# A two-branch gated attention kernel: the row maxima split on VectorE alone, one tile of memory results, other planned times and another order table

## The chip, the cores and the metric

The kernel runs on one NeuronCore of a Trainium2 chip, as one launch. The metric is the device time of an execution in microseconds. The time before is the median of three runs.

## What is computed

Two branches, A and B, with weights of their own, work on the same input x of 2048 tokens by 640 columns (all in fp32). A gate per token mixes their results. Each branch is an attention of 32 heads with 20 columns a head. The tokens are cut into four segments of 512. Inside a segment a head does causal softmax attention; from the segments before, it reads a compressed memory. The core of one branch, cut:

```python
for s in range(4):                       # segments of 512 tokens
    logits = qs @ ks.T * 20 ** -0.5 + mask        # causal
    a_dot = softmax(logits) @ vs
    a_mem = (phi(qs) @ M) / (phi(qs) @ z + 1e-6)
    outs.append(g * a_mem + (1 - g) * a_dot)      # g: one number per head
    M = M + phi(ks).T @ vs
    z = z + sum(phi(ks))
return concat(outs) @ wo
...
gate = sigmoid((x * gate_w).sum(-1))
return gate * A(x) + (1 - gate) * B(x)
```

Here phi(t) is t + 1 for positive t and exp(t) otherwise.

## The kernel before

**Windows and quads.** A window t (0 to 7) is one segment of one branch: segment t // 2, branch t % 2. Its 32 heads are worked on in eight quads of four heads; quads are numbered i = 8 t + u, 64 in all. The names that follow are those of the profile's tiles.

**Products in two parts.** The products by wq, wk, wv and wo need more precision than one pass of TensorE (PE) in its fast fp32 form gives. Each operand is split into a high part (a rounded copy) and a low part (the difference), and three products are summed. Inputs of 64 rows are used, so that the two halves of PE's array work on different matmuls at a time. These matmuls are line 773.

**Scores twice.** For each quad the scores are made in two layouts. S units (`s_unit`, matmuls at line 1209) make them with queries on partitions; VectorE (DVE) adds the causal mask and takes the maximum of each row (line 1196, into the tile `mx`). T units (`t_unit`, matmuls at line 1299) make them with keys on partitions; the maximum goes in as two more rows of the operands, so that ScalarE (ACT) only has to take the exponential (line 1291), after which GpSimd (POOL) clears the block on the diagonal (line 1292). The weighted sum of the values is `pv_unit` (line 1319, 32 matmul records a quad).

**From the maxima to the T units.** When the ten groups of maxima of a quad are there, `m_unit` makes a tile `mt` of 16 + 16 columns: a rounded copy (ACT, line 1220) and the difference (POOL, line 1221). `mrow_unit` transposes it on PE (line 1234), ACT copies it out (line 1251), and two DMAs on the queue of SyncE (SP, line 1246) put it into the last rows of the query operand `qst`. Only then may the quad's T units run.

**From a quad to the output.** The sums of a quad go to DRAM (`dots`). When the eight quads of a window are there, they come back in a layout by head columns: `reciprocals` makes the weights of the rows (line 1379 on DVE, then two reciprocals at line 1384), and `mix` multiplies each of the five pieces by them, on DVE (line 1429) or on POOL (line 1430), whichever the planner thinks free first. For windows 2 to 7 the result of the memory has been written by `mem_unit` into a tile `O` (PE line 883, then three DVE instructions at lines 897, 899 and 900). `o_transpose` turns it (PE line 925) and DVE adds it to the weighed piece (line 1496). The sum is split into two parts (ACT line 1420, then DVE line 1422 or POOL line 1423) and goes into the product by wo. Window 7 does this last part in another way: its quads are turned and weighed one by one (`fin_unit`). A tile `O` is given back when its five transposes are done; there are two of them. `update_unit` adds a window's keys and values to the memory, after that window's memory results have been read.

**Row tiles.** Most tiles of 128 x 512 come from one pool of NBIG = 29 rows (`big`). A T unit may start when there is room for its exponentials: in ten tiles of their own, or in this pool beyond a reserve.

**The order.** The order of all instructions is fixed while the program is made. The kernel's Python code holds a planner: a clock, a queue by priority for each of ACT (A), DVE (D), POOL (G) and SP (S), and a planned duration for each instruction. A line such as `put("D", 0.9, emit, then, prio=2)` says: on DVE, planned for 0.9 us, when done call `then`. `anyof` puts a piece of work on the engine whose queue is the shorter. PE's order comes out of the same clock: a unit is placed when the planner thinks its inputs there. On the chip each engine runs its instructions in the planned order and waits on semaphores wherever reality is later.

**The table.** `RULES` has an entry for a quad i where anything changes: the order of the quad's five S and five T units, then seven numbers that `rules` reads as span (the stretch over which they are spread), calm (the load of DVE up to which late units may start), lag, room (the reserve for exponentials), hold (how much earlier the quad starts), wait and wait2. The numbers hold until the next entry that changes them.

Of the kernel before, what the change touches and what calls it, by code (L numbers as in the profile page):

```python
# [12 lines left out]
F32 = mybir.dt.float32  # L13
# [3 lines left out]
ALU = mybir.AluOpType  # L17

P = 128
D = 640  # L20
S = 2048
# [3 lines left out]
L = 512  # L25
KT = D // P
NB = L // P
# [10 lines left out]
def r32(ap):  # L38
    return ap.bitcast(F32)
# [3 lines left out]
def tile_gated_mix_infini_attn(  # L43
# [17 lines left out]
    nc = tc.nc  # L61
# [7 lines left out]
    sb = ctx.enter_context(tc.tile_pool(name="sb", bufs=2))  # L69
# [18 lines left out]


    RULES = {  # L90
# [60 lines left out]
    }  # L151
    rule = {}
    DONE = {"A": 0.27, "D": 0.26, "G": 0.22, "S": 0.0}
# [46 lines left out]
    def put(e, dur, emit, then=None, prio=5):  # L200
        heapq.heappush(ready[e], (prio, next(seq), dur, emit, then))
        load[e] += dur
        start_next(e)
# [184 lines left out]
    gcol = [const.tile([P, 1], F32, name=f"gcol{b}") for b in range(2)]  # L388


    NBIG, NWST, NWH, SPARE = 29, 3, 4, 2
    VN = D // 2
    bank = Store([ps.tile([P, L], F32, name=f"bank{i}") for i in range(8)])

# [308 lines left out]
    def by_head(t, o):  # L703
        return o.rearrange("p n (h e) -> p n h e", e=DH) if t == 7 else o.rearrange("p n (c h e) -> p n h c e", c=KT, h=H)

    O_store = Store([sb.tile([P, NB, D], F32, tag=f"O{i}", name=f"O{i}", bufs=1) for i in range(2)])
    OTs = {}
    pqTs = {}
    arrived = set()
# [505 lines left out]
    def m_unit(i):  # L1215

        mt = sb.tile([P, 2, 2, 2 * NB], F32R, tag="mt32", name=f"mt{i}", bufs=3)
        m = mx[i].rearrange("p f a n -> p f (a n)")
        mts[i] = mt
        put("A", 0.11, lambda: nc.scalar.copy(mt[:, :, 0, :], m), lambda: put(  # L1220
            "G", 0.18, lambda: nc.gpsimd.tensor_tensor(
                out=mt[:, :, 1, :], in0=m, in1=r32(mt[:, :, 0, :]), op=ALU.subtract),
            lambda: m_ready(i), prio=0), prio=1)

    def m_ready(i):
        m_done.add(i)
        later(0, 0.2, lambda: True, lambda: mrow_unit(i))
# [148 lines left out]

    def reciprocals(t, d, g):
        def gates():
            put("D", 0.9, lambda: nc.vector.scalar_tensor_tensor(
                out=r32(d), in0=r32(d), scalar=gcol[t % 2], in1=r32(g), op0=ALU.mult, op1=ALU.mult), lambda: half(0), prio=2)  # L1380

        def half(c):
            cols = slice(L // 2 * c, L // 2 * (c + 1))
            put("D", 1.78, lambda: nc.vector.reciprocal(r32(d[:, cols]), r32(d[:, cols])),
                (lambda: half(1)) if c == 0 else done, prio=2)
            if c == 0:
                big.give(g)

        def done():
            inverse[t] = d  # L1390
            for fn in waiting.pop(t, []):
                fn()

        landed = then_all(2, gates)
        b = t % 2
        dma(0.8, lambda: nc.sync.dma_start(
            out=r32(d), in_=lanes_of(t)[:, DH:DH + 1, :].to_broadcast([H, 4, L])), landed, prio=-1, lat=1.2)
        dma(0.8, lambda: nc.sync.dma_start(
            out=r32(g), in_=rowg[t // 2][NB * b:NB * b + NB, :].rearrange("n p -> (n p)")[None, :].to_broadcast([P, L])), landed, prio=-1, lat=1.2)
# [4 lines left out]
    def mix(t, k, y):  # L1404
        def weighed():
            weighed_of[t] = weighed_of.get(t, 0) + 1
            if weighed_of[t] == KT:
                big.give(inverse.pop(t))
            if t < 2:
                parts()  # L1410
            else:
                mixed[t, k] = y
                later(1, 0.44, lambda: all(
                    (t, n, h) in mem_done for n in range(NB) for h in range(2)), lambda: o_transpose(t, k, parts))

        def parts():
            big.want((F32R, F32R), two_parts, prio=2)

        def two_parts(hi, lo):
            put("A", 0.515, lambda: nc.scalar.copy(hi, r32(y)), lambda: anyof(  # L1420
                2, lambda: (big.give(y), OTs.__setitem__((t, k), (hi, lo))),
                D=(0.85, lambda: nc.vector.tensor_tensor(out=lo, in0=r32(y), in1=r32(hi), op=ALU.subtract)),  # L1422
                G=(1.25, lambda: nc.gpsimd.tensor_tensor(out=lo, in0=r32(y), in1=r32(hi), op=ALU.subtract))), prio=2)

        def weigh():
            r = inverse[t]
            anyof(
                2, weighed,
                D=(0.9, lambda: nc.vector.tensor_tensor(out=r32(y), in0=r32(y), in1=r32(r), op=ALU.mult)),  # L1429
                G=(1.4, lambda: nc.gpsimd.tensor_tensor(out=r32(y), in0=r32(y), in1=r32(r), op=ALU.mult)))  # L1430

        def landed():
            if t in inverse:
                weigh()
            else:
                waiting.setdefault(t, []).append(weigh)

        dma(0.82, lambda: nc.sync.dma_start(out=r32(y), in_=lanes_of(t)[:, 4 * k:4 * k + 4, :]), landed, prio=0, lat=1.2)
# [353 lines left out]
```

## Time and profile before

| | |
|---|---|
| median of three runs | 1015.88 us (1014.32 to 1016.97) |
| the profiled execution's own time | 1016.54 us |
| its span, first to last instruction | 1014.8 us |
| PE, matmuls | 1002.1 us busy, 11260 matmuls |
| DVE | 769.3 us busy, 2604 instructions |
| ACT | 659.5 us busy, 1341 instructions |
| POOL | 612.3 us busy, 1040 instructions |
| mean granted clock of PE | 0.995 |
| DMA | 241.99 MB, 238 GB/s |

How to read the lines of it: times are in us unless marked ns. A group of instructions has the line of the kernel, the engine, the operation, the tiles it writes and reads (numbers left out), the shape and the count; then the busy time and the mean of one in ns; then the idle time of the engine just before them, with what ended most of it. The view of one line gives the least, the median and the largest duration in ns, and the first and the last start. In the timeline, a row has its start, its length, engine and line; the square bracket is the idle time before it and what ended it. PEld are weight loads, which run beside matmuls. Two matmuls run at a time, one in each half of the array, so PE counts as busy when only one of the halves is.

### The profile page before, as it was taken

What the parts mean: (1) busy time and instruction counts of PE and PEld (TensorE: products, weight loads), DVE (VectorE), ACT (ScalarE), POOL (GpSimd) and SP (SyncE); (2) the same over time, 40 slices, a digit from 0 to 9 for tenths busy, and PEclk for the clock granted to TensorE, in tenths of its full rate; (3) what the DMA queues carried; (4) which work ended last, traced back from release to release, by engine and by line L of the source; (5) the groups of instructions that cost most, each with busy time, mean ns of one, the idle gap of its engine ahead of it and who ended that gap; (6) DMA issues with size and microseconds to landing.
All of it is one profiled execution on the core that took longest, in us unless ns stands there. A gap on an engine that the chain in (4) does not pass through costs nothing.

```text
span 1014.8 us, 30827 instructions
## 1 busy us (share of the span) xinstructions
PE 1002.1 (99%) x11260; PEld 855.5 (84%) x11260; DVE 769.3 (76%) x2604; ACT 659.5 (65%) x1341; POOL 612.3 (60%) x1040
## 2 busy tenths in 40 slices
PE   9999999999999999999999999999999999999998
PEld 7998888888888888878888878897889888878876
DVE  4688777976787778877578976888567897689764
ACT  5376776776566767757766666675676666675672
POOL 4465657676476655775646656486675656567571
PEclk9999999999999999999999999998999999999999
DMA  7999989898896988866768687795876979688531
GB/s 248 308 306 270 298 255 305 274 283 259 262 286 185 286 237 245 268 183 219 237 177 300 188 267 234 206 301 175 252 230 182 313 213 281 206 228 267 151 93 62
DMA packets 148886, 241.99 MB, mean 238 GB/s; under 512 B 13216, under 2 KB 46144, under 8 KB 148416
## 3 DMA queue, kind: packets, MB, share of 16 engines
q1 hardware_dynamic: 148736, 240.03, 77.2%
q8 instruction: 89, 1.46, 0.6%
q14 instruction: 61, 0.50, 0.2%
HBM read 150.83 MB, written 94.65 MB: 242 GB/s over the span
## 4 chain that ended last, share of the span: by engine, by line
PE 84%; DMA 6%; DVE 5%; ACT 1%; POOL 1%; issue 1%; SPq 1%; ACTq 0%; DVEq 0%; POOLq 0%
PE bank L773 50%; PE bank L1319 13%; PE bank L1299 7%; PE bank L1209 7%; PE bank L883 3%; PE bank L965 3%; PE bank L925 2%; DMA row<-dots 1%; DMA dots<-row 1%; DMA kd<-row 1%; DVE bank L1196 1%; PE bank L1234 1%; DVE row L1429 1%; DVE row L1422 1%; DMA row<-in_xT_dram 1%
## 5 line engine op out<-in xcount | busy, mean ns | idle before, releaser
L1196 DVE CUSTOM_DVE_ANT_0 bank<-bank,tri 128x256 f32<-128x256 f32 (+3 forms) x1024 | 474.7, 520 | 150.2 <-PE bank L1209 96.8
L773 PE MATMUL bank<-row,wh 64*128 64x512 f32 x2308 | 498.6, 403 | 0.6 <-DVE mw L897 0.6
L1291 ACT ACTIVATE p<-bank 128x512 f32<-128x512 f32 x588 | 324.0, 601 | 140.0 <-PE bank L1299 108.4
L1292 POOL TENSOR_SCALAR_AFFINE_SELECT p<-p 128x256 f32<-128x256 f32 (+1 forms) x588 | 219.2, 380 | 228.6 <-ACT p L1291 219.2
L773 PEld LDWEIGHTS bank<-row,wh 64*128 64x128 f32 x2308 | 319.8, 186 | 11.8 <-issue 1.1
L773 PE MATMUL bank<-row,wl 64*128 64x512 f32 x1154 | 293.3, 402 | 0.0
L543 POOL TENSOR_TENSOR wl<-wst,wh 128x640 fp32r<-128x640 f32 x115 | 181.3, 1581 | 58.1 <-ACT wh L541 51.7
L1209 PE MATMUL bank<-kst,qst 60*128 60x384 f32 (+3 forms) x1024 | 184.0, 317 | 1.8 <-DVE row L1349 0.8
L773 PEld LDWEIGHTS bank<-row,wl 64*128 64x128 f32 x1154 | 173.6, 186 | 5.0 <-issue 0.6
L1299 PE MATMUL bank<-qst,kst 62*128 62x128 f32 (+3 forms) x1024 | 176.4, 317 | 1.0 <-ACT vst L1015 0.5
L773 PE MATMUL bank<-wvh,row 64*128 64x320 f32 x1280 | 176.7, 312 | 0.0
L1319 PE MATMUL bank<-p,vst 128*32 128x384 f32 (+3 forms) x1936 | 148.9, 431 | 0.0
L773 PEld LDWEIGHTS bank<-wvh,row 64*128 64x128 f32 x1280 | 147.4, 185 | 1.0 <-issue 0.2
L1196 DVE DVE_READ_ACCUMULATOR2_ANT mx<- 128x1 f32 x1024 | 144.6, 141 | 0.0
L1209 PEld LDWEIGHTS bank<-kst,qst 60*128 60x128 f32 x1024 | 137.5, 186 | 8.2 <-DVE row L1349 1.2
L1299 PEld LDWEIGHTS bank<-qst,kst 62*128 62x128 f32 x1024 | 130.5, 186 | 7.3 <-DVE mx L1196 1.0
L1319 PEld LDWEIGHTS bank<-p,vst 128*32 128x32 f32 x1936 | 59.3, 110 | 87.4 <-issue 62.7
L541 ACT CAST wh<-wst 128x640 fp32r<-128x640 f32 x119 | 86.4, 741 | 20.2 <-PE bank L773 14.4
L773 PE MATMUL bank<-wvl,row 64*128 64x320 f32 x640 | 99.3, 310 | 0.0
L1349 ACT COPY row<-bank 128x512 f32<-128x512 f32 x61 | 36.0, 590 | 79.4 <-PE bank L1319 71.1
L773 PEld LDWEIGHTS bank<-wvl,row 64*128 64x128 f32 x640 | 80.0, 185 | 0.6 <-issue 0.4
L518 POOL TENSOR_TENSOR wvl<-wst,wvh 128x640 fp32r<-128x640 f32 (+1 forms) x48 | 64.0, 1338 | 17.3 <-ACT wvh L515 17.3
(117 smaller groups left out, 1213.5 us busy)
## 6 DMA issues: line engine op xcount, KB each, us to landing
qst<-qd SPq DMA_DIRECT2D x128, 240.0 KB
kst<-kd SPq DMA_DIRECT2D x128, 240.0 KB
qd<-row SPq DMA_DIRECT2D x40, 512.0 KB
kd<-row SPq DMA_DIRECT2D x40, 512.0 KB
dots<-row SPq DMA_DIRECT2D x56, 256.0 KB
wst<-wmix SPq DMA_DIRECT2D x35, 320.0 KB
row<-dots SPq DMA_DIRECT2D x42, 256.0 KB
qd<-row SPq DMA_DIRECT2D x40, 256.0 KB
```

The source lines that it names most:

```text
L518: put("G", 0.77 * n, lambda: nc.gpsimd.tensor_tensor(out=wl[:, a:b, :], in0=w3, in1=r32(wh[:, a:b, :]), op=ALU.subtract), end, prio=4)
L541: put("A", 0.625, lambda: nc.scalar.copy(wh, w3), lambda: put(lo_eng, lo_cost, lambda: lo.tensor_tensor(out=wl, in0=w3, in1=r32(wh), op=AL ...
L543: lambda: lo.tensor_tensor(out=wl, in0=w3, in1=r32(wh), op=ALU.subtract), end, prio=3), prio=6)
L773: return nc.tensor.matmul(bank_of, lhsT=w[ROWS[half]], rhs=x_[ROWS[half]], start=start, stop=stop)
L883: return nc.tensor.matmul(pm[:, a - h0:c - h0, :].rearrange("p h e -> p (h e)"), lhsT=r32(pqTs[t, m][ROWS[half], P * n:P * (n + 1)]), rhs= ...
L1196: put("D", w / 960.0 + 0.105, lambda: nc.vector.tensor_tensor_reduce(out=sc[:, off:off + w], in0=sc[:, off:off + w], in1=tri[:, L - w:], s ...
L1209: lane_ops[half].append((mm(w), lambda pair=pair, qb=qb, off=off, w=w, r=r, sc=sc: nc.tensor.matmul(sc[:, off:off + w], lhsT=q[r, pair, P ...
L1291: put("A", 0.483, lambda: nc.scalar.activation(pt, sc, AF.Exp, scale=SCALE), lambda: (bank.give(sc), put("G", 0.15 + 0.105 * len(todo), la ...
L1292: "G", 0.15 + 0.105 * len(todo), lambda: nc.gpsimd.affine_select(out=blocks, in_=blocks, pattern=[[0, len(todo)], [1, P]], base=0, channel ...
L1299: lane_ops[half].append((mm(w), lambda pair=pair, kb=kb, off=off, w=w, r=r, sc=sc: nc.tensor.matmul(sc[:, off:off + w], lhsT=k[r, pair, P ...
L1319: nc.tensor.matmul(po[32 * j:32 * j + 32, P * kb:], lhsT=vst[t % 2][:, kb, h * E1:h * E1 + 32], rhs=pts[i, n, f][0][:, off:off + w], start ...
L1349: either(0.483, lambda: nc.scalar.copy(r32(oT), po), 0.605, lambda: nc.vector.tensor_copy(r32(oT), po), end, 2)
```

## The change

Four things at once:

- `m_unit` makes both parts of the maxima on DVE, as one planned step of 0.22 us at the first priority (0): a copy of the 16 columns, then the subtraction. Before, the copy was a step of ACT and the subtraction one of POOL.
- There is one tile `O` in place of two, and the pool of rows has 34 in place of 29.
- Planned durations of five steps are larger: the gates of `reciprocals` on DVE, 0.9 to 1.0; the low part in `two_parts`, DVE 0.85 to 0.95 and POOL 1.25 to 1.35; the weighing in `mix`, DVE 0.9 to 1.05 and POOL 1.4 to 1.5. The instructions themselves stay.
- The table `RULES` is another one: 56 entries in place of 60, four of them shared.

With each of these the planner comes to another order, so the instructions of all engines stand in a new order. The diff, its table cut to a few entries:

```diff
     RULES = {
-        0: "TSTSTSTSTS 0.933 2.38 0.30 4 0.0 3.08 1",
-        1: "TSTSTSTSTS 1.010 2.38 0.27 8 0.0 1.6 1.60",
-        2: "TSTSTSTSTS 1.036 2.04 0.30 6 0.0 1.6 0.40",
...
+        0: "TSTSTSTSTS 1.033 2.38 0.30 8 0.0 1.6 1.41",
+        1: "TSTSTSTSTS 0.953 3.71 0.30 8 0.0 2.99 0.36",
+        2: "TTSTSTSTSS 1.010 3.52 0.30 4 0.0 2.63 0.25",
...
     }
...
-    NBIG, NWST, NWH, SPARE = 29, 3, 4, 2
+    NBIG, NWST, NWH, SPARE = 34, 3, 4, 2
...
-    O_store = Store([sb.tile([P, NB, D], F32, tag=f"O{i}", name=f"O{i}", bufs=1) for i in range(2)])
+    O_store = Store([sb.tile([P, NB, D], F32, tag=f"O{i}", name=f"O{i}", bufs=1) for i in range(1)])
...
-        put("A", 0.11, lambda: nc.scalar.copy(mt[:, :, 0, :], m), lambda: put(
-            "G", 0.18, lambda: nc.gpsimd.tensor_tensor(
-                out=mt[:, :, 1, :], in0=m, in1=r32(mt[:, :, 0, :]), op=ALU.subtract),
-            lambda: m_ready(i), prio=0), prio=1)
+
+        def parts():
+            nc.vector.tensor_copy(mt[:, :, 0, :], m)
+            nc.vector.tensor_tensor(out=mt[:, :, 1, :], in0=m, in1=r32(mt[:, :, 0, :]), op=ALU.subtract)
+
+        put("D", 0.22, parts, lambda: m_ready(i), prio=0)
...
-            put("D", 0.9, lambda: nc.vector.scalar_tensor_tensor(
+            put("D", 1.0, lambda: nc.vector.scalar_tensor_tensor(
...
-                D=(0.85, lambda: nc.vector.tensor_tensor(out=lo, in0=r32(y), in1=r32(hi), op=ALU.subtract)),
-                G=(1.25, lambda: nc.gpsimd.tensor_tensor(out=lo, in0=r32(y), in1=r32(hi), op=ALU.subtract))), prio=2)
+                D=(0.95, lambda: nc.vector.tensor_tensor(out=lo, in0=r32(y), in1=r32(hi), op=ALU.subtract)),
+                G=(1.35, lambda: nc.gpsimd.tensor_tensor(out=lo, in0=r32(y), in1=r32(hi), op=ALU.subtract))), prio=2)
...
-                D=(0.9, lambda: nc.vector.tensor_tensor(out=r32(y), in0=r32(y), in1=r32(r), op=ALU.mult)),
-                G=(1.4, lambda: nc.gpsimd.tensor_tensor(out=r32(y), in0=r32(y), in1=r32(r), op=ALU.mult)))
+                D=(1.05, lambda: nc.vector.tensor_tensor(out=r32(y), in0=r32(y), in1=r32(r), op=ALU.mult)),
+                G=(1.5, lambda: nc.gpsimd.tensor_tensor(out=r32(y), in0=r32(y), in1=r32(r), op=ALU.mult)))
```

102 rows, old and new, of the table RULES are left out of this document.

## The prediction

> **What bounds the kernel now.** I read the page first, then the clock and the waits of TensorE (PE), then stretches of the span side by side, and last the two worst stretches instruction by instruction.
>
> ```profile
> span 1014.8 us, 30827 instructions
> PE 1002.1 (99%) x11260; PEld 855.5 (84%) x11260; DVE 769.3 (76%) x2604; ACT 659.5 (65%) x1341; POOL 612.3 (60%) x1040
> core 0: 1014.8 us, clock 0.995
> PE bank L1234 <- POOL mt L1221: 1.6, 1, 1.6
> ```
>
> TensorE has a matmul in flight for 1002.1 of 1014.8 us and the change gives it no matmul more or less. So only three things can move the time: idle time of PE (12.7 us), time at a lowered clock (0.005 of 1014.8, 5.1 us), and how closely the order packs matmuls into the two halves of the array, which a busy share of 99% hides. The longest wait of PE that ended on another engine is the last line: the transposes of the maxima stood 1.6 us behind GpSimd (POOL), once. The stretches say where the losses lie (columns: stretch, length, then busy time and instructions of PE, weight loads, DVE, ACT and POOL, granted clock, DMA share, GB/s):
>
> ```profile
> 120.00:220.00 100.00, 99.39 (x1139) 85.01 (x1138) 79.47 (x264) 72.84 (x151) 65.16 (x107) 1.00 0.91 285
> 220.00:320.00 100.00, 99.22 (x1165) 85.99 (x1162) 76.50 (x253) 65.41 (x135) 61.09 (x104) 1.00 0.83 253
> 420.00:440.00 20.00, 17.86 (x209) 14.85 (x209) 18.46 (x55) 14.08 (x30) 15.05 (x21) 0.96 0.83 261
> 440.00:460.00 20.00, 20.00 (x214) 17.48 (x214) 12.66 (x46) 10.83 (x22) 13.00 (x25) 0.95 0.57 176
> 540.00:600.00 60.00, 59.12 (x697) 50.40 (x695) 52.90 (x161) 37.17 (x74) 36.05 (x60) 1.00 0.77 232
> 680.00:700.00 20.00, 19.21 (x211) 15.04 (x209) 17.69 (x54) 12.21 (x26) 14.16 (x17) 0.83 0.74 227
> 920.00:940.00 20.00, 19.49 (x258) 16.87 (x257) 19.30 (x57) 12.54 (x25) 16.08 (x19) 1.00 0.71 211
> 1000.00:1015.00 15.00, 10.34 (x61) 7.92 (x57) 7.43 (x13) 0.91 (x2) 0.00 (x0) 1.00 0.25 87
> ```
>
> The last row holds 4.66 us of the idle time and is the tail, where the last product waits for its last inputs; the change does not touch it. The other rows hold 0.61 + 0.78 + 2.14 + 0.88 + 0.79 + 0.51 = 5.71 us. The clock costs 20 x 0.04 + 20 x 0.05 + 20 x 0.17 = 5.2 us in the rows with 0.96, 0.95 and 0.83, all of what the mean of 0.995 says. So 10.9 us are lost in the middle, nearly all at the same place of the work: where the attention results of a window have come back from DRAM, are weighed by reciprocals, and transposes add the memory results. There DVE is at 18.46, 17.69 and 19.30 of 20 us. The two costliest places, from the timeline and from the chain:
>
> ```profile
> 435.91 0.62 ACT L586 CAST row<-row 128x512 fp32r<-128x512 f32 x1 [2.16 <-DMA row<-in_xT_dram]
> 436.43 0.20 ACT L1220 CAST mt<-mx 128x16 fp32r<-128x16 f32 x1
> 436.71 0.22 POOL L1221 TENSOR_TENSOR mt<-mx,mt 128x16 fp32r<-128x16 f32 x1 [1.52 <-ACT mt L1220]
> 436.98 0.23 PE L1234 MATMUL bank<-ident,mt 64*32 64x64 f32 x1 [1.59 <-POOL mt L1221]
> ```
>
> ```profile
> 672.02 2.29 PE bank L1319 x32
> ...
> 685.28 1.79 DVE row L1429
> ...
> 691.40 3.79 PE bank L1319 x32
> ```
>
> First place: ScalarE's queue is in order and its next instruction waited for a DMA; the small copy of the maxima (L1220) stood behind it, POOL stood idle 1.52 us for the copy, PE 1.59 us for POOL. No arithmetic was late, only a queue that had nothing to do with the maxima. Second place: PE runs short behind one weighing (L1429) of 1.79 us on the chain, and afterwards the same 32 matmuls take 3.79 us where they take 2.29 elsewhere: the lowered clock. A stall here costs its idle time and then as much again in clock.
>
> **The change, part by part.** The rows for it:
>
> ```profile
> L1220 ACT CAST mt<-mx 128x16 fp32r<-128x16 f32 x64 | 13.6, 212 | 17.2 <-DVE mx L1196 16.6 <-DVE mw L897 0.6
> L1221 POOL TENSOR_TENSOR mt<-mx,mt 128x16 fp32r<-128x16 f32 x64 | 16.5, 258 | 19.9 <-ACT mt L1220 16.4 <-PE bank L1319 3.4
> L897 DVE SCALAR_TENSOR_TENSOR mw<-bank,gq 128x19 f32<-128x19 f32 (+1 forms) x48 | 8.1, 168 | 9.4 <-PE bank L883 9.4
> L1468 DVE TENSOR_TENSOR fw<-bank,gqd 128x16 f32<-128x16 f32 x8 | 1.3, 162 | 4.8 <-PE bank L1234 3.6 <-PE bank L925 1.1
> L1496 DVE TENSOR_TENSOR row<-bank,row 128x512 f32<-128x512 f32 x25 | 15.7, 682 | 3.4 <-PE bank L925 3.0 <-POOL wl L543 0.3
> L1422 DVE TENSOR_TENSOR row<-row,row x16: 678/1170/1790, 186.4 to 930.8; 128x512 fp32r<-128x512 f32 x16
> L1429 DVE TENSOR_TENSOR row<-row,row x12: 689/1288/1924, 185.2 to 920.9; 128x512 f32<-128x512 f32 x12
> ```
>
> *Maxima on DVE.* Removed: 64 copies of 212 ns from ACT (13.6 us) and 64 subtractions of 258 ns from POOL (16.5 us). Neither engine is the bound, so this frees queues, not time. Also gone are the two handovers. Added: two instructions of 16 columns on DVE for each of 64 quads. The trace has no such pair on DVE; the nearest rows are L1468 (16 columns, 162 ns) and L897 (19 columns, 168 ns), so 0.33 us a quad, 21 us in all, DVE from 769 to 790 us (78%). I take this value. The upper bound is given by two DVE rows with both inputs in SBUF: L1422 and L1429 take 678 and 689 ns at the least, as L1496 does whose one input is in PSUM (682), but up to 1790 and 1924. So such an instruction can lose 1.1 to 1.2 us; both of a pair losing that would be 64 x 2 x 1.2 = 154 us, which no row comes near on average: L1422's median is 0.49 over its least, so 64 x 2 x 0.49 = 63 us is the end I keep.
>
> The Trainium skill ("SBUF — State Buffer", section "Who interferes with whom") speaks against the move: a VectorE instruction with two SBUF inputs and a GpSimd instruction that reads SBUF exclude each other, and whichever comes second blocks for the other's whole length. The spread of L1422 and L1429 agrees; L1496's mean of 682 does too. By that rule the subtraction would often wait for POOL, and the sum would carry rival 2's price instead of the 0.33.
>
> What queues behind the pair on DVE (it has the first priority there): the next quad's score scans (L1196), whose end frees score banks for PE. Its only waits are for the scans before it, on its own engine, and for the transposes of three quads earlier to have read the buffer. The two DMAs that carry the transposed maxima keep their count and stay on SP. The stall at 435 goes: -1.59 us, and its lowered clock (0.8 + 1.0), together **-3.4 us**. Late next is what PE runs behind the transposes: scores from 437.17 on and the first output product, whose rows POOL (L1423) still splits until 442; it stands later in the order, so it is covered.
>
> *Corrected row times.* The instructions do not change, only where the planner puts the PE work that needs them. Rows for the rest:
>
> ```profile
> L1379 DVE SCALAR_TENSOR_TENSOR row<-row,gcol,row 128x512 f32<-128x512 f32 x7 | 7.4, 1053 | 6.7 <-DMA row<-rowg 5.4 <-DMA kst<-kd 1.3
> L1422 DVE TENSOR_TENSOR row<-row,row 128x512 fp32r<-128x512 f32 x16 | 18.2, 1148 | 0.0
> L1423 POOL TENSOR_TENSOR row<-row,row 128x512 fp32r<-128x512 f32 x19 | 26.5, 1400 | 10.4 <-ACT row L1420 9.7 <-ACT mr L1251 0.6
> L1429 DVE TENSOR_TENSOR row<-row,row 128x512 f32<-128x512 f32 x12 | 15.3, 1291 | 0.0
> L1430 POOL TENSOR_TENSOR row<-row,row 128x512 f32<-128x512 f32 x23 | 31.9, 1406 | 7.1 <-DVE row L1384 5.2 <-DVE fw L1468 1.9
> ```
>
> Planned before: 0.9, 0.85, 1.25, 0.9, 1.4. Unplanned work: 7 x 0.15 + 16 x 0.30 + 19 x 0.15 + 12 x 0.39 + 23 x 0.01 = 13.6 us, about 1.9 in each of the seven weighings. With 1.0, 0.95, 1.35, 1.05, 1.5 it is 7 x 0.05 + 16 x 0.20 + 19 x 0.05 + 12 x 0.24 - 23 x 0.09 = 5.3 us, 0.8 in each. More than half of the surprise goes, so I take half of the stalls that lie there: half of 4.2 us at 680 (0.79 idle, 3.4 clock) and half of 0.61 + 0.78 + 0.88 + 0.51 = 2.8: **-3.5 us**. Bounds: none of it, or all 7.0.
>
> *DVE's new work inside the weighings.* At DVE's 17.7 to 19.3 of 20 us nothing hides it there. 64 quads over 1014.8 us are 1.3 in 20 us, so 0.43 us in each of seven, 3 us; the shorter chain of the maxima pays half: **+1.5 us**.
>
> *One tile of memory results.* The tile (4 x 640 floats a partition) makes place for exactly the five rows that the pool grows by. The memory results of the next window can then be written only after the transposes have read the present ones:
>
> ```profile
> L900 DVE TENSOR_TENSOR O<-bank,mw x4: 553/554/554, 371.8 to 384.0; 128x380 f32<-128x380 f32 x4
> L925 PE MATMUL bank<-ident,O x40: 216/222/273, 421.7 to 434.7; 64*128 64x64 f32 x40
> L899 DVE RECIPROCAL mw<-mw 128x19 f32<-128x19 f32 (+1 forms) x48 | 12.4, 258 | 1.6
> ```
>
> Four results (L900) were written at 372 to 384 while the tile before was read only at 422 to 435. They must move 50 us later; their inputs hold two rows longer and the two keys' rows whose update follows them, four of the five new ones. No row shows a PE wait on this, before the change; I take 0, because their only successor is the memory's update, and keep rival 1's price as the upper bound.
>
> *New table.* It reorders scores, products and filling between them. No row prices an order not run. Lower bound: the whole 10.9 us lost in the middle; upper bound: another stall as at 420 to 460 (2.1 idle + 1.8 clock) in each of three more windows, +12. I take 0.
>
> Sum against the profiled execution, 1016.54 us (span 1014.8, 1.74 around it): 1016.54 - 3.4 - 3.5 + 1.5 = 1011.1. The median of the runs, 1015.88, lies 0.66 lower, so **1010.5 us**.
>
> **The rivals.**
> 1. *The single tile brings a queue* (slower). Half a window's memory units fall into the time after the transposes: 4 x (0.168 + 0.258 + 0.554) = 3.9 us of DVE, in five windows (third to seventh), 19.6 us. For: DVE is nearly full exactly there. Against: PE has other products to run. It decides where PE's order has those units or their updates ahead of ready work. With half covered: 1010.5 + 9.8 = 1020.3; with none, 1030.
> 2. *DVE and POOL get into each other's way* over the pair (slower). 63 us more on DVE is 769 + 21 + 63 = 853 us, 84%, still below PE, so it shows in the weighings only: 1.3 quads x 0.98 us x seven = 8.9 us: 1019.4. For: the spread of L1422. Against: POOL is busy 60%, much of it with short masks.
> 3. *The stalls only move*: the next late input takes the place, the time stays within 3 us of 1015.9. For: POOL and DVE have the same weighing work as before.
> 4. *The order packs better as well*: most of the 10.9 us go and the five rows let score exponentials run ahead: about 1003.
>
> **How the numbers follow.** About 0.3% (3 us) can be told from no change, so faster means below 1012.8, slower above 1018.9. Forecast 0.48, rival 4 0.11, rival 3 0.14, rival 1 0.17, rival 2 0.10. Faster 0.48 + 0.11 = 0.59, the same 0.14, slower 0.27. The forecast's own range is 1005 to 1013 (bounds of the row times and of the pair). For 8 in 10 I leave out the better part of rival 4, below 1001, and the uncovered part of rival 1, above 1024.
>
> **What would show it.** Right: no ACT or POOL instruction on the maxima, 128 small DVE ones near 0.17 us; no wait of PE on them; granted clock at 1.00 in every stretch and PE's idle time near 9 us or less. Wrong: a row of 0.4 us or more for the pair's subtraction (rival 2); long waits of memory units or DVE at 20 of 20 us behind the transposes (rival 1); the clock still below 0.9 somewhere with another weighing in front of it (rival 3).

## The result, and the profile after

The changed kernel takes 1017.86 us, the median of 17 runs; the kernel before, run beside it, takes 1014.32 us, also the median of 17 runs. The ratio is 1.0031, with a 95% interval of 1.0021 to 1.0040. So it is slower by about 3.1 us by the ratio (3.5 us by the medians): little, but clear of the noise, where 1010.5 us and a gain were forecast.

The page of the changed kernel, its clock, and its longest wait of PE on another engine. (Its lines are numbered 2 to 4 lower than those of before: 1218 and 1219 are the pair of the maxima, L1205 and L1297 the two kinds of scores.)

```profile
span 1016.6 us, 30789 instructions
core 0: 1016.6 us, clock 1.000
PE 1002.2 (99%) x11260; PEld 855.9 (84%) x11260; DVE 814.0 (80%) x2732; ACT 654.1 (64%) x1281; POOL 596.3 (59%) x972
PE bank L1232 <- DVE mt L1219: 1.6, 4, 0.5
```

The handover from ACT and POOL is gone: 60 instructions fewer on ACT, 68 on POOL, and 128 more on DVE (64 left ACT and POOL each with the maxima; the rest is the new plan's choice of engine). But DVE is busy 44.7 us longer, not 21, and PE is idle for 14.4 us (1016.6 - 1002.2), not 9 or less. PE's busy time is the same as before (1002.2 against 1002.1 us), though the mean granted clock of this execution is 1.000 where it was 0.995. So the 5.1 us that the lowered clock had cost were won and lost again: at full clock the same matmuls now keep PE busy about 5 us longer. The stretches, in the columns of the prediction:

```profile
320.00:420.00 100.00, 98.58 (x1106) 83.11 (x1102) 79.87 (x277) 63.65 (x127) 59.99 (x100) 1.00 0.86 261
420.00:440.00 20.00, 20.00 (x231) 18.67 (x231) 17.52 (x49) 16.12 (x31) 17.55 (x20) 1.00 0.81 250
440.00:460.00 20.00, 20.00 (x250) 17.53 (x251) 18.33 (x64) 11.00 (x21) 9.86 (x19) 1.00 0.62 183
600.00:680.00 80.00, 78.34 (x885) 65.96 (x877) 63.95 (x206) 53.69 (x108) 48.59 (x72) 1.00 0.81 250
680.00:700.00 20.00, 19.35 (x221) 15.69 (x217) 19.17 (x52) 11.72 (x23) 13.80 (x18) 1.00 0.96 299
800.00:920.00 120.00, 118.47 (x1320) 99.38 (x1319) 102.95 (x337) 74.41 (x145) 70.62 (x115) 1.00 0.80 242
```

At the two costliest places of before there is no idle time at 420 to 460 and 0.65 us at 680 to 700 (0.79 before), and the clock there is 1.00. New idle time stands elsewhere, 1.42 us at 320 to 420, 1.66 us at 600 to 680 and 1.53 us at 800 to 920, where before had none. What the pair takes, by groups and then by its least, median and longest:

```profile
L1219 DVE TENSOR_TENSOR mt<-mx,mt 128x16 fp32r<-128x16 f32 x64 | 26.4, 413 | 2.2
L1218 DVE CAST mt<-mx 128x16 fp32r<-128x16 f32 x64 | 23.2, 362 | 0.8
L1218 DVE CAST mt<-mx x64: 161/175/1465, 40.7 to 983.3; 128x16 fp32r<-128x16 f32 x64
L1219 DVE TENSOR_TENSOR mt<-mx,mt x64: 174/176/1525, 41.0 to 983.5; 128x16 fp32r<-128x16 f32 x64
```

More than half of these instructions, 78 of 128, take 0.16 to 0.20 us, about the forecast 0.17. The other 50 take up to 1.5 us for 16 columns. So the pair's mean is 362 + 413 = 775 ns a quad, 49.6 us in all, against 0.33 us forecast and 0.22 us planned. One of the long pairs, in the timelines of POOL, DVE and PE:

```profile
783.72 1.55 POOL L539 TENSOR_TENSOR wl<-wst,wh 128x640 fp32r<-128x640 f32 x1 [0.33 <-ACT wh L537]
785.23 0.88 POOL L514 TENSOR_TENSOR wvl<-wst,wvh 128x320 fp32r<-128x320 f32 x1
...
784.16 1.14 DVE L1218 CAST mt<-mx 128x16 fp32r<-128x16 f32 x1
785.33 0.80 DVE L1219 TENSOR_TENSOR mt<-mx,mt 128x16 fp32r<-128x16 f32 x1
786.06 0.68 DVE L719 TENSOR_TENSOR row<-bank,row 128x512 f32<-128x512 f32 x1
...
786.79 0.44 PE L1205 MATMUL bank<-kst,qst 60*128 60x384 f32 x1 [0.70 <-DVE row L719]
```

The copy begins while POOL splits a weight, and ends at 785.30, when POOL's instruction ends (785.27). POOL's next begins at 785.23; the subtraction ends with it, at 786.13 against 786.11. The eviction that stood behind the pair (L719) comes late, and PE waits 0.70 us for its bank. This is one piece of the loss from end to end.

It is no single case: in this trace each of the 50 instructions of the pair that take more than 0.2 us ends 22 to 34 ns after the end of an instruction of POOL that had begun before it.

### The profile page after: what moved, and what is told of

It reads as the page before. It is cut to its first block, busy times and chain, and to the rows that moved or that the text cites. A ratio compares the mean times of both kernels' runs of the same rounds, so it can differ in the third digit from the quotient of the medians.

```text
span 1016.6 us, 30789 instructions
## 1 busy us (share of the span) xinstructions
PE 1002.2 (99%) x11260; PEld 855.9 (84%) x11260; DVE 814.0 (80%) x2732; ACT 654.1 (64%) x1281; POOL 596.3 (59%) x972
## 4 chain that ended last, share of the span: by engine, by line
PE 86%; DVE 7%; DMA 3%; ACT 1%; issue 1%; SPq 0%; POOL 0%; DVEq 0%; ACTq 0%
PE bank L769 51%; PE bank L1317 12%; PE bank L1297 7%; PE bank L1205 7%; PE bank L961 3%; PE bank L879 3%; PE bank L921 2%; DVE bank L1192 2%; DMA row<-rowg 1%; PE bank L1232 1%; DVE mt L1218 1%; DVE mt L1219 1%; DVE row L735 1%; DVE row L1494 1%; ACT p L1289 1%
## 5 line engine op out<-in xcount | busy, mean ns | idle before, releaser
L1192 DVE CUSTOM_DVE_ANT_0 bank<-bank,tri 128x384 f32<-128x384 f32 (+3 forms) x1024 | 474.5, 519 | 125.3 <-PE bank L1205 99.4
L769 PE MATMUL bank<-row,wh 64*128 64x512 f32 x2308 | 517.6, 404 | 1.1 <-DMA qst<-qd 0.8
L1289 ACT ACTIVATE p<-bank 128x512 f32<-128x512 f32 x566 | 311.1, 600 | 127.2 <-PE bank L1297 95.5
L1290 POOL TENSOR_SCALAR_AFFINE_SELECT p<-p 128x128 f32<-128x128 f32 (+1 forms) x566 | 214.0, 386 | 237.7 <-ACT p L1289 225.4
L769 PEld LDWEIGHTS bank<-row,wh 64*128 64x128 f32 x2308 | 324.8, 185 | 12.3 <-DVE mx L1192 1.2
L769 PE MATMUL bank<-row,wl 64*128 64x512 f32 x1154 | 296.7, 399 | 0.0
L539 POOL TENSOR_TENSOR wl<-wst,wh 128x640 fp32r<-128x640 f32 x115 | 179.4, 1565 | 52.7 <-ACT wh L537 51.9
L1297 PE MATMUL bank<-qst,kst 62*128 62x128 f32 (+3 forms) x1024 | 179.7, 318 | 2.7 <-DVE row L1494 0.7
L1205 PE MATMUL bank<-kst,qst 60*128 60x128 f32 (+3 forms) x1024 | 179.0, 317 | 1.7 <-DVE row L719 0.7
L1317 PE MATMUL bank<-p,vst 128*32 128x512 f32 (+3 forms) x1888 | 144.7, 424 | 0.0
L1297 PEld LDWEIGHTS bank<-qst,kst 62*128 62x128 f32 x1024 | 132.1, 186 | 11.8 <-DVE mx L1192 1.8
L1205 PEld LDWEIGHTS bank<-kst,qst 60*128 60x128 f32 x1024 | 131.2, 186 | 8.2 <-DVE mx L1192 1.8
L769 PE MATMUL bank<-wvl,row 64*128 64x320 f32 x640 | 103.4, 311 | 0.0
```

What stands on the lines that cost most here:

```text
L539: lambda: lo.tensor_tensor(out=wl, in0=w3, in1=r32(wh), op=ALU.subtract), end, prio=3), prio=6)
L769: return nc.tensor.matmul(bank_of, lhsT=w[ROWS[half]], rhs=x_[ROWS[half]], start=start, stop=stop)
L1192: put("D", w / 960.0 + 0.105, lambda: nc.vector.tensor_tensor_reduce(out=sc[:, off:off + w], in0=sc[:, off:off + w], in1=tri[:, L - w:], s ...
L1205: lane_ops[half].append((mm(w), lambda pair=pair, qb=qb, off=off, w=w, r=r, sc=sc: nc.tensor.matmul(sc[:, off:off + w], lhsT=q[r, pair, P ...
L1289: put("A", 0.483, lambda: nc.scalar.activation(pt, sc, AF.Exp, scale=SCALE), lambda: (bank.give(sc), put("G", 0.15 + 0.105 * len(todo), la ...
L1290: "G", 0.15 + 0.105 * len(todo), lambda: nc.gpsimd.affine_select(out=blocks, in_=blocks, pattern=[[0, len(todo)], [1, P]], base=0, channel ...
```

## The experiments

Two theories were put against each other. **P**: the unplanned length of the pair on DVE made the kernel slower. **O**: the new order packs worse on the chip, wherever the pair runs. The kernels of experiments 1 to 8 keep the planner's numbers of the kernel they start from, so PE's order stays what it was and only the instructions on the other engines differ.

**1. The changed kernel with the parts on ACT and POOL again.**

```diff
-            nc.vector.tensor_copy(mt[:, :, 0, :], m)
-            nc.vector.tensor_tensor(out=mt[:, :, 1, :], in0=m, in1=r32(mt[:, :, 0, :]), op=ALU.subtract)
+            nc.scalar.copy(mt[:, :, 0, :], m)
+            nc.gpsimd.tensor_tensor(out=mt[:, :, 1, :], in0=m, in1=r32(mt[:, :, 0, :]), op=ALU.subtract)
```

> The changed kernel with its order of TensorE untouched (the planner still counts 0.22 us of VectorE for the maxima), but the copy is issued on ScalarE and the subtraction on GpSimd, as before the change. In the changed kernel's profile the pair takes 362 + 413 ns a quad, 49.6 us in all, where the planner counts 0.22 us a quad, 14 us. Theory P (the unplanned length of the pair on VectorE is what made it slower): the 3.5 us come back, 1013 to 1015 us. Theory O (the new order itself packs worse on the chip, wherever the pair runs): 1017 to 1019 us, as the changed kernel.

Measured: 1013.47 us, ratio to before 0.9979 (0.9967 to 0.9991). All of the loss comes back, and 2.1 us more: theory P.

**2. The kernel before with the pair on DVE.**

```diff
-        put("A", 0.11, lambda: nc.scalar.copy(mt[:, :, 0, :], m), lambda: put(
-            "G", 0.18, lambda: nc.gpsimd.tensor_tensor(
...
+        put("A", 0.11, both, lambda: put("G", 0.18, lambda: None, lambda: m_ready(i), prio=0), prio=1)
```

`both` issues the copy and the subtraction on DVE.

> The kernel before with its order of TensorE untouched, but both parts of the maxima are issued on VectorE at the place of the ScalarE copy. Theory P: slower by about 3 us or more, 1017 to 1020 us, the pair near 0.8 us a quad. Theory O: no change beyond 1 us, 1013.5 to 1015.5 us.

Measured: 1024.52 us, ratio 1.0100 (1.0081 to 1.0120); the pair takes 405 + 405 = 810 ns a quad. Theory P again, and the loss of 10 us is larger than the 3 or more expected. The old order counts nothing on DVE for the pair, the new one 0.22 us; that this makes the difference is likely, but no run shows it.

```profile
L1221 DVE CAST mt<-mx 128x16 fp32r<-128x16 f32 x64 | 25.9, 405 | 0.7
L1222 DVE TENSOR_TENSOR mt<-mx,mt 128x16 fp32r<-128x16 f32 x64 | 25.9, 405 | 2.2
```

**3. The pair twice in a row, in the changed kernel** (the two lines of the pair stand twice).

> The changed kernel with the pair on VectorE issued twice in a row (the second writes the same values again); order of TensorE untouched. VectorE gets about another 25 to 50 us. Theory P: another 3 to 4 us slower, about 1021 us. Theory O: within 1.5 us of the changed kernel, 1017 to 1019.5 us.

Measured: 1045.02 us, ratio 1.0298 (1.0280 to 1.0316). Theory P by its sign. The 41.8 us more on DVE (855.8 against 814.0) lie in the 25 to 50 expected, but they cost 27 us and not 3 to 4. PE now waits 13.3 us for the maxima, in 12 waits:

```profile
PE 1011.2 (97%) x11260; PEld 863.4 (83%) x11260; DVE 855.8 (82%) x2860; ACT 654.8 (63%) x1281; POOL 594.7 (57%) x972
PE bank L1234 <- DVE mt L1221: 13.3, 12, 2.9
```

**4. The pair in a form that reads one input at most.**

```diff
-            nc.vector.tensor_copy(mt[:, :, 0, :], m)
-            nc.vector.tensor_tensor(out=mt[:, :, 1, :], in0=m, in1=r32(mt[:, :, 0, :]), op=ALU.subtract)
+            nc.vector.tensor_reduce(out=mt[:, :, 0, :], in_=m[:, :, :, None], axis=mybir.AxisListType.X, op=ALU.max)
+            nc.vector.memset(r32(mt[:, :, 1, :]), 0.0)
```

> The changed kernel with the same two places on VectorE, but the copy is a reduction over an axis of length one and the subtraction a fill with zeros, so that no instruction of the pair reads two inputs from SBUF (the low part of the maxima is left out). If the long cases of the pair come from GpSimd at work beside it, both instructions now take 0.15 to 0.2 us each time, the longest under 0.4 us, and VectorE's busy time falls by 25 us or so. Theory P then gives back two thirds of the loss: about 1015.5 us. Theory O: 1017 to 1019 us.

Measured: 1009.82 us, ratio 0.9952 (0.9935 to 0.9968). The page, the pair's groups and three of the stretches:

```profile
PE 997.9 (99%) x11260; PEld 857.7 (85%) x11260; DVE 778.3 (77%) x2732; ACT 653.4 (65%) x1281; POOL 594.3 (59%) x972
L1218 DVE TENSOR_REDUCE mt<-mx 128x16 fp32r<-128x16 f32 x64 | 10.5, 165 | 0.8
L1219 DVE MEMSET mt<- 128x16 f32 x64 | 4.6, 72 | 0.0
600.00:680.00 80.00, 79.19 (x888) 67.82 (x885) 61.25 (x214) 54.86 (x111) 48.83 (x75) 1.00 0.84 258
680.00:700.00 20.00, 19.94 (x242) 18.04 (x239) 18.74 (x53) 13.72 (x27) 16.62 (x20) 1.00 0.79 252
800.00:920.00 120.00, 119.46 (x1364) 101.69 (x1362) 100.17 (x358) 78.05 (x152) 74.30 (x116) 1.00 0.82 245
```

The long cases are gone, and DVE is busy 35.7 us less. From 1.0031 to 0.9952 this is worth 0.0079, 8.0 us: more than theory P's 2.4, because the loss against before had hidden a gain of the new order. Of the 8.9 us between the two profiled spans (1016.6 and 1007.7) about half is idle time of PE (14.4 to 9.8 us); the other half is busy time of the same matmuls at the same full clock (1002.2 to 997.9), which the share of 99% doesn't tell. POOL's busy time hardly moves (596.3 to 594.3 us, and its splits of weights, line 539, take 1565 and 1564 ns): what shows in these meetings is DVE waiting, not POOL.

**5. The high part alone.** The fill of experiment 4 is not repeated; three tiles with a zero low part are kept from the start.

```diff
-        mt = sb.tile([P, 2, 2, 2 * NB], F32R, tag="mt32", name=f"mt{i}", bufs=3)
+        mt = mtz[i % 3]
...
-            nc.vector.tensor_copy(mt[:, :, 0, :], m)
-            nc.vector.tensor_tensor(out=mt[:, :, 1, :], in0=m, in1=r32(mt[:, :, 0, :]), op=ALU.subtract)
+            nc.vector.tensor_reduce(out=mt[:, :, 0, :], in_=m[:, :, :, None], axis=mybir.AxisListType.X, op=ALU.max)
```

> The changed kernel, order of TensorE untouched; of the pair only the rounded copy is left, as a reduction over an axis of length one, and the low part is a zero that is written once at the start (any shift of a softmax row is exact as long as both sums use it, so the rounded maximum alone will do). Against the run with a fill (1009.8 us), 72 ns a quad less on VectorE, 4.6 us in all. Theory P: 1008.5 to 1010 us. A rest of the new order's own (theory O) would show as no further gain, 1009.5 to 1010.5.

Measured: 1010.19 us, ratio 0.9957 (0.9942 to 0.9973). The same as experiment 4 within the intervals: the further gain that theory P asked for (1008.5 to 1010 us) did not come, and the time lies in theory O's range. With one instruction of 164 ns a quad, it is a kernel that beats both, and leaves nothing out that the softmax needs.

**6. The pair as long as in the changed kernel, but always equally long.** Two longer reductions and the fill:

```diff
-            nc.vector.tensor_copy(mt[:, :, 0, :], m)
-            nc.vector.tensor_tensor(out=mt[:, :, 1, :], in0=m, in1=r32(mt[:, :, 0, :]), op=ALU.subtract)
+            for n in (15, 10):
+                nc.vector.tensor_reduce(
+                    out=mt[:, :, 0, :], in_=m[:, :, :, None].to_broadcast([P, 2, 2 * NB, n]), axis=mybir.AxisListType.X, op=ALU.max)
+            nc.vector.memset(r32(mt[:, :, 1, :]), 0.0)
```

> The changed kernel, order of TensorE untouched; the pair is three instructions that read one input at most and take together about 0.78 us, as long as the pair's mean in the changed kernel, but every time the same (low part left out). Theory L (the mean length on VectorE is what costs): as the changed kernel, 1017 to 1019 us. Theory W (the waits cost because they come where GpSimd and VectorE are both full, up to 1.5 us at once): 1012 to 1015 us.

Measured: 1015.11 us, ratio 1.0000 (0.9987 to 1.0013); the pair takes 2 x 358 + 72 = 788 ns a quad. It falls between the two theories, just above W's range.

```profile
L1219 DVE TENSOR_REDUCE mt<-mx 128x16 fp32r<-128x240 f32 (+1 forms) x128 | 45.8, 358 | 3.0
L1221 DVE MEMSET mt<- 128x16 f32 x64 | 4.6, 72 | 0.0
```

Read so, of the 8.0 us between experiment 4 and the changed kernel 4.9 us (0.0048) come from the mean length, and 3.1 us (0.0031) from its coming in waits of up to 1.5 us. Both shares are clear of zero, but by the intervals each is known to about 2 us only.

**7. The kernel before with the short pair on DVE** (the pair of experiment 4 at the place of experiment 2).

> The kernel before, order of TensorE untouched, with the pair of the 1009.8 us run on VectorE: a reduction of 165 ns and a fill of 72 ns in place of the ScalarE copy and the GpSimd subtraction (low part left out). The stall of 1.6 us at 435 us and its lowered clock should go, as the prediction priced them (3.4 us): 1011 to 1012.5 us; then the new order is worth only 1 to 2 us. If it stays at 1014 to 1015.5, the handovers cost nothing and the new order is worth 5 us.

Measured: 1015.24 us, ratio 1.0008 (0.9995 to 1.0021). No net gain: taking the handovers away, priced at 3.4 us in the prediction, and putting 15 us of unplanned work on DVE come out even. The profile of this run shows why the stall did not go. ScalarE waits for the same transfer again, and the next instruction behind it, another copy, keeps PE waiting in place of the maxima (L1300 is the second kind of scores):

```profile
433.72 0.62 ACT L586 CAST row<-row 128x512 fp32r<-128x512 f32 x1 [1.57 <-DMA row<-in_xT_dram]
434.25 0.58 ACT L941 COPY row<-bank 128x512 f32<-128x512 f32 x1
434.88 0.57 PE L1300 MATMUL bank<-qst,kst 62*128 62x512 f32 x2 [1.10 <-ACT row L941]
680.00:700.00 20.00, 18.91 (x208) 14.32 (x206) 18.38 (x59) 11.57 (x23) 14.21 (x17) 0.91 0.64 199
```

With the same pair the new order is worth 0.9952 against 1.0008, 5.7 us. With the parts on ACT and POOL it is worth 2.1 us (experiment 1 against before), with the long pair 7.0 us (the changed kernel against experiment 2): each order was planned for one place of the pair, so its worth has no single number.

**8. Only the copy in the one-input form**, the subtraction as in the changed kernel.

```diff
-            nc.vector.tensor_copy(mt[:, :, 0, :], m)
+            nc.vector.tensor_reduce(out=mt[:, :, 0, :], in_=m[:, :, :, None], axis=mybir.AxisListType.X, op=ALU.max)
```

> The changed kernel, order of TensorE untouched; only the copy is replaced by the reduction over an axis of length one, the subtraction with its two inputs from SBUF stays, and nothing is left out. If each of the two waited for GpSimd on its own account, the copy falls from 362 to 165 ns, the subtraction stays near 413 ns or rises a little, the pair costs 0.58 to 0.65 us a quad, and half of the 8 us comes back: 1012.5 to 1015 us. If the copy's waits only move on to the subtraction, the pair stays at 0.7 us or more and the time at 1016 to 1018 us.

Measured: 1014.85 us, ratio 0.9991 (0.9974 to 1.0007): 4.1 of the 8 us are back, and the pair takes 164 + 426 = 590 ns a quad, as expected if each of the two waits on its own account.

```profile
L1218 DVE TENSOR_REDUCE mt<-mx x64: 151/163/171, 40.3 to 978.0; 128x16 fp32r<-128x16 f32 x64
L1219 DVE TENSOR_TENSOR mt<-mx,mt x64: 174/177/1595, 40.5 to 978.2; 128x16 fp32r<-128x16 f32 x64
```

The reduction never takes more than 171 ns, in a place where the copy took up to 1465. The subtraction still takes up to 1595.

**9. The kernel before, profiled once more.**

> The kernel before, unchanged, for a second profile of it. Theory S (the two stalls priced in the prediction belong to the kernel): an idle time of TensorE of 1 us or more near 435 us that ends on GpSimd's part of the maxima, and a clock below 0.97 at 420 to 460 us and below 0.9 at 680 to 700 us. Theory V (they belong to the one execution that was profiled): at least one of the two, or the lowered clock, is missing or elsewhere, while the execution's time is within 3 us of the other.

Measured: one execution of 1015.09 us, span 1013.4 us. Its stretches at the places of the two stalls:

```profile
420.00:440.00 20.00, 19.46 (x231) 16.32 (x229) 19.37 (x57) 14.90 (x32) 16.49 (x23) 1.00 0.82 261
440.00:460.00 20.00, 20.00 (x226) 18.05 (x224) 13.41 (x50) 11.36 (x23) 12.19 (x25) 1.00 0.64 191
680.00:700.00 20.00, 18.91 (x196) 14.22 (x195) 17.43 (x52) 10.96 (x22) 13.54 (x15) 0.83 0.68 206
```

Theory V for the first place: 0.54 us idle in place of 2.14, at full clock, and no wait for the maxima is in the list of PE. ScalarE's wait for the transfer, 2.16 us in the first profile, is short here:

```profile
434.41 0.62 ACT L586 CAST row<-row 128x512 fp32r<-128x512 f32 x1 [0.36 <-DMA row<-in_xT_dram]
```

Theory S for the second: 1.09 us idle and a clock of 0.83, as in the first profile.

**10 to 12. One part undone.** Experiment 10 takes back the five planned durations, 11 the table, 12 the single tile and the 34 rows. Here the order is planned anew.

> The changed kernel with the five planned durations of before (0.9, 0.85, 1.25, 0.9, 1.4); no instruction is another, only the planned times and so the order. Theory A (the parts add up, and the new order's 5 to 6 us come from the row times): 1019 to 1024 us. Theory B (the table fits only the plan it was made with, and any other plan loses its order): 30 us slower or more, above 1045 us, with TensorE's wait spread over many quads and the row times' own worth not to be read from it.

> The changed kernel with the table of the kernel before. Theory A (parts add up): 1013 to 1024 us. Theory B (a table fits one plan): above 1045 us.

> The changed kernel with two tiles of memory results and 29 rows, as before. Theory A with the single tile as a loss (the prediction's first rival): 1008 to 1014 us; with the five rows as a gain: 1019 to 1025 us. Theory B: above 1045 us.

Measured, in two runs each: 1060.18 us (ratio 1.0447, 1.0382 to 1.0511), 1064.51 us (1.0489, 1.0426 to 1.0552) and 1071.45 us (1.0558, 1.0486 to 1.0629). Theory B: the table fits only the plan that it came with. Experiment 10 changes only five planned numbers, and the planner then puts ten more instructions on DVE and orders all of them anew. The expected wait of PE is not what grows most: its idle time is 20.7 us (1059.2 - 1038.5) against 14.4, while the same matmuls keep it busy for 36.3 us longer.

```profile
PE 1038.5 (98%) x11260; PEld 880.3 (83%) x11260; DVE 819.7 (77%) x2742; ACT 649.7 (61%) x1276; POOL 587.4 (55%) x967
```

So none of the three parts has a price of its own that such a run could show, and which of them the 5.7 us of the new order are owed to stays open.

## Why the prediction was wrong, step by step

**The pair's size is the step that failed.** The prediction took 0.33 us a quad from the rows of L1468 and L897. Both of these read PSUM for one input; the pair has its inputs in SBUF only, and the right rows stood beside them, L1422 and L1429 with their spread. They were kept as an upper bound of 63 us for 64 quads, on top of 21. Measured were 49.6 us in all, 29 above the 21, and this decides the sign: with the pair at 0.24 us (experiment 4) the kernel is at 1009.82 us, with the real pair at 1017.86. The term "+1.5 us" for DVE's new work lacked these 8.0 us: it went by DVE's mean load in the weighings and left out that an instruction of the pair is at times held up for over a microsecond. Nor did the sum count the third thing that the prediction had named, how closely the matmuls are packed: about half of the 8.9 us between the profiles of experiment 4 and the changed kernel is busy time of PE.

**Rival 2 was what happened.** Its chance of 0.10 was far too small. That its price of 8.9 us is close to the 8.0 measured is partly luck: it took 63 us more on DVE where 29 came, and charged them in the weighings only, while the new idle time also stands between them (1.1 us at 600 to 672 us, before the weighing that begins at 674). The reason against it, that POOL's work is much of it short masks, was a count and not a sum of time: the splits of weights, 1565 ns each, are 115 of 972 POOL instructions but 179 of its 596 us, and a pair that meets one waits up to 1.5 us.

```profile
L539 POOL TENSOR_TENSOR wl<-wst,wh 128x640 fp32r<-128x640 f32 x115 | 179.4, 1565 | 52.7 <-ACT wh L537 51.9 <-POOL p L1290 0.4 <-PE bank L1317 0.3
```

The rule that the prediction quotes from the Trainium skill ("SBUF — State Buffer", section "Who interferes with whom") was the better guide. Experiments 4 and 8 agree with it for the subtraction, whose long cases go with its second SBUF input. By the same section of the Trainium skill a copy from SBUF can, depending on its operands, use the ports shared with GpSimd as well, and a reduction never does on this chip. The runs agree, 1465 ns at the longest for the copy against 171 for the reduction; the prediction had applied the rule to the subtraction alone.

**The stall at 435 us, -3.4 us, was not there to be had.** Its cause is ScalarE's wait for a transfer, as the prediction read it, but the wait differs between executions: 2.16, 0.36 and 1.57 us in three profiles of the old order. And where it is long, taking the maxima out of ScalarE's queue only puts the next instruction in their place (1.10 us of PE in experiment 7): at this place rival 3 was right. The depth of it belonged to the one execution that the prediction priced. Whether the handovers cost something elsewhere stays open: in the new order the short pair on DVE (experiment 4) is about 2.7 us faster than the parts on ACT and POOL (experiment 1), but that order's plan does not count the parts there.

**The corrected row times, -3.5 us.** The place at 680 us behaved as argued, above all in its clock: 0.79 us idle and a clock of 0.83 before (1.09 and 0.83 in the second profile, 1.09 and 0.91 in experiment 7), 0.65 us idle and a clock of 1.00 after, 0.06 and 1.00 in experiment 4. It is no chance of one execution: the mean granted clock of the kernel before is 0.9965 over the 52 runs beside the experiments (0.993 to 0.998), that of the changed kernel 0.9995 over its 17 runs (0.998 to 1.000). Counted as the prediction counts the clock, the 0.003 are 3 us of 1015. Whether the row times did it or the table cannot be told (experiments 10 to 12). For the new order as a whole, table, tile and times together, 5.7 us were measured with the short pair where -3.5 stood in the sum. That 1010.5 lies so near to experiment 4 is partly luck: one step promised 3.4 us for a stall that did not go, another 2.2 too little.

**Rival 1 did not show.** In the changed kernel two lines of PE's waits name the memory tile, 0.3 and 0.2 us, and experiment 4 beats the kernel before with the single tile in place. The direct trial of two tiles (experiment 12) lost the order and says nothing on it.

```profile
PE bank L769 <- DVE O L896: 0.3, 1, 0.3
PE bank L1297 <- DVE O L896: 0.2, 1, 0.2
```

**The signs named ahead.** No ACT or POOL instruction on the maxima: right. 128 DVE instructions near 0.17 us: right by the medians (175 and 176 ns), wrong by the means, and the mark set for rival 2, 0.4 us or more for the subtraction, was met with 413 ns. No wait of PE on the maxima: wrong, 1.6 us in four waits. PE's idle time near 9 us or less: wrong, 14.4. Clock at 1.00: right. DVE near 20 of 20 us behind the transposes, the mark of rival 1, was nearly met (19.17 at 680 to 700), but the pair alone brings it down (18.74 in experiment 4).

## What to carry to other kernels

Price a small instruction that moves to DVE by a row with the same kinds of operands, SBUF or PSUM, and by its mean and longest duration, not by a row of the same length or by the median; where POOL runs instructions of 1.5 us beside it, two inputs in SBUF, or a plain copy from SBUF, can cost several times their own length. A stall seen in one profiled execution is worth its price only if a second profile shows it at the same place; and ask what else stands in the queue behind the late transfer before counting it as gone. Where an order was tuned for one plan, test a part by keeping the order and changing only the instructions; undoing it in the plan measures the lost tuning.

## What the runs showed that was not expected

- DVE's time has no fixed price: between experiment 4 and the changed kernel 0.22 us of time for each us of DVE (8.0 for 35.7), between the changed kernel and experiment 3 0.65 (27 for 41.8), though DVE is busy for no more than 82% of the span. Whether it is how full DVE is, or the length of the one step in which the doubled pair stands, no run separates.
- About half of what the pair cost shows nowhere as idle time of PE: the same 11260 matmuls keep it busy for 1002.2 us in the changed kernel and 997.9 us in experiment 4, both at full clock.
- A reduction over an axis of length one is a copy that was never held up: 164 ns in the mean for 128 x 16, 171 at the longest, beside a copy with a mean of 362.
- The low part of the maxima is not needed: the shift of a softmax row cancels as long as both sums use it, and dropping it saves an instruction a quad (experiment 5).
